# Routing attention and a snake MLP on one core: the first head's one-hot rows made by TensorE, and the preparation of the first pairs dealt out anew

## The chip, the core and the metric

The kernel runs on one core of one Trainium2 chip. The metric is the time of one execution on the device in microseconds (us).

The engines have short names in the profile. PE is TensorE's matmuls, PEld its weight loads, DVE is VectorE, ACT is ScalarE, POOL is GpSimd, and SP is the queue that issues DMAs. "PE S L358" is line 358 of a kernel writing a tile S. The change adds lines near the top of the file, so the same statement has another line number before and after:

| statement | before | after |
|---|---|---|
| scores, two matmuls | L326, L327 | L358, L359 |
| exp | L332 | L364 |
| probabilities times v | L341 | L373 |
| scaling of the attention output to `xs` | L353 | L385 |
| hidden layer | L425 | L457 |
| output layer | L394 | L426 |
| transposes of q and k; their copies by DVE and by ACT | L144; L150, L154 | L144; L150, L154 |
| copies of one-hot rows, by ACT and by DVE | none | L337, L339 |

## The reference, cut to what matters

```python
batch, n_heads, seq, head_dim = (4, 8, 768, 64); n_clusters = 16
q_assign = argmax(einsum('bhsd,hcd->bhsc', q_n, c_n)); k_assign = argmax(...)   # normalised
mask   = q_assign[:, :, :, None] == k_assign[:, :, None, :]
scores = where(mask, scale * q @ k.T, -1e9)
attn   = softmax(scores) @ v                  # x: (3072, 512)
h = x @ w_in                                  # 512 -> 2048
s = sin(alpha * h); g = h + s * s / (alpha + 1e-9)
out = g @ w_out                               # 2048 -> 512
```

Every query and key is assigned to the nearest of 16 centroids. A query sees only the keys of its own cluster.

## The kernel before

The kernel works on 16 pairs of heads, four per batch. A pair takes 12 steps: one block of 128 keys of one head each. A step is a scores product on PE, an exp on ACT, and the product with v on PE. After 48 steps the batch changes to its second part, the MLP, with Sin instead of exp. The next batch's attention follows.

The mask costs no instruction in the loop. Below the 64 rows of q and k in the tile `QK`, 16 rows hold the one-hot assignment, and the scores product adds them. Making these rows is the preparation of a pair. It consists of four PE transposes of q and k, four copies to `T32`, an assignment product, a transpose on DVE, a maximum, a comparison that gives `oh`, a transpose back and DMA moves into `QK`.

```python
def prep_T(m, g, bk=None, eng="dve"):        # one of four: head g//2, q or k
    for jj in range(NJ2):
        nc.tensor.transpose(out=bk[:, P * jj : P * jj + P], ...)          # L144
    if eng == "dve":
        nc.vector.tensor_scalar_mul(out=s["T32"][:, g, :], ...)           # L150
    else:
        nc.scalar.activation(out=s["T32"][:, g, :], ..., func=Copy)       # L154

def head_move(m, h, engs):                   # one-hot rows of one head into QK by DMA
    for g in range(4):
        engs[t].dma_start(out=QK[D : D + NHC, ...], in_=s["ohT"][...])
```

The entry handles pair 0 head by head, so that the first scores start early. Pair 1's transposes follow in the time in which the first head's moves are on the way:

```python
    head_asn(0, 0, M0)
    prep_cast(0, 0)
    for i in range(4):
        prep_hot(0, i, QS)
    prep_T(0, 2, SA[0][:, 0:512], "act")
    prep_T(0, 3, M1, "act")
    head_move(0, 0, [nc.sync, nc.scalar])
    ...
    head_move(0, 1, [nc.sync, nc.sync])
    prep_T(1, 0, M2, "act")
    prep_T(1, 2, M1)
    prep_T(1, 1, M0, "act")
    prep_T(1, 3, OB)
```

Everything else of batch 0 is placed at a step by a table. A row holds the pair, its four transposes with their steps, the step of its assignment, and the steps of its two casts:

```python
    for m, make, asn, cast in (
        (1, (), 1, (0, 0)),
        (2, ((0, 4), (2, 5), (1, 6), (3, 7)), 8, (7, 8)),
        (3, ((0, 12), (1, 14), (2, 16), (3, 17)), 20, (14, 18)),
        ...
```

The change of part, with the transpose `x_T` of the last pair's output, is the same in all four batches:

```python
        hidden_mm(0, A[0], KX - 2, KX - 1)
        hidden_mm(1, A[1], 0, KX - 1)
        x_T(last, OB)
        hidden_mm(2, A[2], 0, KX - 1)
        own = [(1, OB, 3), (0, M0, 5)]       # output products: tile, bank, lag in steps
        for f in range(NF):
            ...
```

The softmax here doesn't subtract the row's maximum and nothing guards it: scores larger than these inputs give would overflow.

## Time and profile before

The median is 312.23 us in the three runs given with the kernel (311.94 to 313.45). The profiled execution spans 310.5 us.

The page's table of engines: busy time, share of the span, and instructions.

```profile
PE 302.7 (97%) x2750; PEld 180.0 (58%) x2750; DVE 208.6 (67%) x367; ACT 239.7 (77%) x324; POOL 139.3 (45%) x222
```

The list of PE's waits, cut to two: engine, tile and line, what was waited for, us in total, times, longest.

```profile
PE S L326 <- DMA QK<-ohT: 1.2, 2, 0.9
PE S L425 <- DVE gT L450: 0.6, 1, 0.6
```

PE is the engine with no room. Its two visible waits that a schedule could remove are the DMA that brings the first one-hot rows (0.9 us, and 0.35 us for pair 1's) and one at the change of part.

The entry in PE's timeline of the kernel before (start us, us busy, what, count, and in brackets the idle time before it with what ended it):

```profile
9.99 0.49 PE L144 MATMUL OB<-ident_f,k 128*128 128x128 f32 x3
10.32 0.38 PE L501 MATMUL S<-gT 128*128 128x512 bf16 x1
11.57 0.38 PE L326 MATMUL S<-QK 80*128 80x512 bf16 x1 [0.86 <-DMA QK<-ohT]
```

The first scores start at 11.57 us, when the DMA has landed.

### The profile page before, as it was taken

The numbers are of one execution on the slowest core, as the hardware profiler recorded it, in microseconds if no ns is written. First come the engines' busy times: TensorE is split into PE (matmuls) and PEld (weight loads), VectorE is DVE, ScalarE is ACT, GpSimd is POOL, SyncE is SP. The second block draws the span as 40 slices with busy tenths as digits, with TensorE's granted clock in tenths as the row PEclk, the third lists the DMA queues.
The fourth block names the chain that finished last, engine by engine and source line by source line (L and its number), as shares of the span: only waits on it lengthen the run. The fifth ranks groups of instructions, "written<-read, shape, count | busy, mean of one in ns | idle before, by whom it ended". The sixth has DMA issues, their size and how long they took to land.

```text
span 310.5 us, 7224 instructions
## 1 busy us (share of the span) xinstructions
PE 302.7 (97%) x2750; PEld 180.0 (58%) x2750; DVE 208.6 (67%) x367; ACT 239.7 (77%) x324; POOL 139.3 (45%) x222
## 2 busy tenths in 40 slices
PE   8899999999999999999999999999999999999995
PEld 4467766455456656555556556555556666555544
DVE  3787796698866876687967877687836312677821
ACT  5689989787689998688679998687679999687300
POOL 5879999019405099985006079990001090000000
PEclk9999999999999999999999999999999999999999
DMA  7459999949653578881044576520011111000031
GB/s 234 142 164 288 310 205 183 200 76 304 219 142 78 116 183 187 256 317 53 0 119 113 104 171 140 143 84 2 0 68 50 37 43 45 6 28 2 0 135 68
DMA packets 28673, 38.91 MB, mean 125 GB/s; under 512 B 5072, under 2 KB 22496, under 8 KB 28640
## 3 DMA queue, kind: packets, MB, share of 16 engines
q0 software_dynamic: 10240, 21.11, 25.9%
q1 hardware_dynamic: 18160, 17.30, 20.6%
q8 instruction: 21, 0.34, 0.4%
q10 hardware_dynamic: 240, 0.06, 0.1%
q14 instruction: 12, 0.10, 0.1%
HBM read 27.30 MB, written 6.29 MB: 108 GB/s over the span
## 4 chain that ended last, share of the span: by engine, by line
PE 87%; ACT 5%; DVE 4%; DMA 2%; issue 1%; SPq 0%; ACTq 0%; DVEq 0%
PE M L394 19%; PE S L425 17%; PE S L326 13%; PE OB L341 10%; PE M L425 8%; PE S L327 6%; PE OB L394 5%; PE M L214 3%; ACT pT L332 3%; PE S L394 2%; DMA QK<-ohT 2%; PE M L144 2%; DVE gT L450 2%; ACT s_sb L438 1%; DVE u_sb L446 1%; PE S L501 1%
## 5 line engine op out<-in xcount | busy, mean ns | idle before, releaser
L332 ACT ACTIVATE pT<-S 128x768 bf16<-128x768 f32 x192 | 143.7, 810 | 15.9 <-PE S L327 14.7
L394 PE MATMUL M<-w_out_bf,gT 128*128 128x512 bf16 (+1 forms) x288 | 90.7, 373 | 0.2
L326 PE MATMUL S<-QK 80*128 80x512 bf16 x192 | 72.9, 380 | 1.5 <-DMA QK<-ohT 1.2
L425 PEld LDWEIGHTS <-w_in_bf 128*128 128x128 bf16 x512 | 49.3, 98 | 37.9 <-issue 1.8
L341 PEld LDWEIGHTS <-pT 128*128 128x128 bf16 x1152 | 56.1, 97 | 21.2 <-ACT pT L332 0.4
L425 PE MATMUL S<-xT,w_in_bf 128*128 128x512 bf16 x352 | 65.0, 326 | 0.7 <-DVE gT L450 0.6
L341 PE MATMUL OB<-VX,pT 128*128 128x65 bf16 x1152 | 61.3, 193 | 0.4 <-ACT pT L332 0.3
L438 ACT ACTIVATE s_sb<-S,alpha_col 128x768 bf16<-128x768 f32 (+2 forms) x45 | 39.4, 886 | 23.7 <-PE S L425 16.1
L394 PEld LDWEIGHTS <-gT 128*128 128x128 bf16 x400 | 38.9, 97 | 30.7 <-issue 5.4
L191 POOL TENSOR_SCALAR QK<-T 64x384 bf16<-64x384 f32 x64 | 35.3, 552 | 37.4 <-DMA T<-Tq 33.4
L327 PE MATMUL S<-QK 80*128 80x256 bf16 x192 | 51.9, 270 | 0.0
L450 DVE SCALAR_TENSOR_TENSOR gT<-u_sb,ralpha,S 128x768 bf16<-128x768 bf16 (+2 forms) x45 | 44.7, 996 | 10.0 <-ACT u_sb L443 7.1
L387 POOL DMA_DIRECT2D xT<-xq x48 | 25.8, 546 | 29.0 <-DVE xq L379 28.1
L425 PE MATMUL M<-xT,w_in_bf 128*128 128x512 bf16 (+1 forms) x160 | 29.9, 326 | 0.0
L186 POOL CAST QK<-T 64x768 bf16<-64x768 f32 x32 | 26.9, 842 | 6.4 <-ACT T L154 3.8
L352 DVE RECIPROCAL rec<-OB 128x6 f32<-128x6 f32 x32 | 6.2, 193 | 34.7 <-PE OB L341 34.7
L446 DVE TENSOR_TENSOR u_sb<-s_sb 128x768 bf16<-128x768 bf16 (+2 forms) x41 | 23.7, 579 | 7.0 <-ACT s_sb L438 7.0
L327 PEld LDWEIGHTS <-QK 80*128 80x128 bf16 x192 | 18.8, 98 | 16.0 <-issue 1.8
L203 POOL CAST VX<-v 128x768 bf16<-128x768 f32 x16 | 13.8, 862 | 28.6 <-issue 27.7
L438 ACT ACTIVATE s_sb<-M,alpha_col 128x512 bf16<-128x512 f32 (+1 forms) x40 | 20.9, 574 | 7.2 <-PE M L425 7.2
L450 DVE SCALAR_TENSOR_TENSOR gT<-u_sb,ralpha,M 128x512 bf16<-128x512 bf16 (+1 forms) x40 | 22.8, 611 | 5.2 <-ACT u_sb L443 4.8
L394 PE MATMUL OB<-w_out_bf,gT 128*128 128x512 bf16 (+1 forms) x80 | 26.2, 358 | 0.1
(83 smaller groups left out, 283.0 us busy)
## 6 DMA issues: line engine op xcount, KB each, us to landing
T<-Tq SPq DMA_DIRECT2D x64, 96.0 KB, 2.5
out_dram<-o_sb SPq DMA_DIRECT2D x23, 256.0 KB, 2.1
v<-in_v_dram POOLq DMA_DIRECT2D x14, 384.0 KB, 4.3
q<-in_q_dram POOLq DMA_DIRECT2D x13, 384.0 KB, 5.5
k<-in_k_dram POOLq DMA_DIRECT2D x13, 384.0 KB, 6.3
w_in_bf<-in_moe_w_in_dram POOLq DMA_DIRECT2D x4, 512.0 KB, 7.2
w_out_bf<-in_moe_w_out_dram POOLq DMA_DIRECT2D x4, 512.0 KB, 9.3
xT<-xq POOLq DMA_DIRECT2D x48, 24.0 KB, 2.3
```

The source lines that it names most:

```text
L186: nc.gpsimd.tensor_copy(out=QK[0:D, m % NQK, h, :, HS * par : HS * par + HS], in_=src)
L191: nc.gpsimd.tensor_scalar(out=QK[0:D, m % NQK, h, t].rearrange("c (n i a) -> c i n a", i=4, a=32)[:, 2 * par : 2 * par + 2], in0=src[:, t] ...
L326: nc.tensor.matmul(out=dst[:, 0:512], lhsT=lhsT, rhs=T[:, 0, 0:512], start=True, stop=True)
L327: nc.tensor.matmul(out=dst[:, 512:S], lhsT=lhsT, rhs=T[:, 0, 512:S], start=True, stop=True)
L332: nc.scalar.activation(out=pT, in_=area(i)[:, 0:S], func=ACTF.Exp, scale=escale)
L341: nc.tensor.matmul(out=o3[:, j, :], lhsT=pT[:, P * j : P * j + P], rhs=VX[m % NVX][:, h, jof(m // NHP, kt), :], start=(kt == 0 and j == 0) ...
L387: nc.gpsimd.dma_start(out=xT[32 * g : 32 * g + 32, 0:2, QS * i : QS * i + QS], in_=xq[0].rearrange("p (h g n) -> p h g n", h=2, g=4)[32 * ...
L394: nc.tensor.matmul(out=bk[:, lo:hi], lhsT=gT[:, f, P * mt : P * mt + P], rhs=w_out_bf[:, f, lo:hi], start=(f == 0), stop=(f == NF - 1),)
L425: nc.tensor.matmul(out=ar[lo // 512][:, 0 : hi - lo] if isinstance(ar, tuple) else ar[:, lo:hi], lhsT=lhsT, rhs=xT[:, kk, :].rearrange("c ...
L438: nc.scalar.activation(out=s_sb[:, lo:hi], in_=src, func=ACTF.Sin, scale=alpha_col[:, f : f + 1])
L446: nc.vector.tensor_tensor(out=u_sb[:, lo:hi], in0=s_sb[:, lo:hi], in1=s_sb[:, lo:hi], op=ALU.mult)
L450: nc.vector.scalar_tensor_tensor(out=gT[:, f, lo:hi], in0=u_sb[:, lo:hi], scalar=ralpha[:, f : f + 1], in1=src, op0=ALU.mult, op1=ALU.add,)
```

## The change

The intent is to start the first scores earlier. PE turns pair 0's first one-hot rows itself, and ACT and DVE copy them into `QK`. The two DVE transposes and the DMA with its wait are gone. The warm-up product that filled this wait goes too. Pair 1 is now handled head by head over steps 0 to 8 and no longer in the entry, so the rest of the table moves back. At the change of part the last pair's `x_T` goes forward, and bank OB's lag in batch 0 becomes 4. The diff, cut to its core:

```diff
-        dense = m < NPE and W == HS
+        dense = m < NPE and W == HS and m != 2        # pair 2: the other layout, four moves
+    def head_rows(m, h, bks):          # 12 PE transposes of oh, then six copies
+        for par in range(2):
+            ... nc.tensor.transpose(out=bk[...], in_=oh[:, par, i, 0:NHC], identity=ident_b)
+        put(0, 0, both, 0, n, "act")
+        put(1, 0, 0, 0, 4, "dve")
+        put(0, 1, both, 0, n, "dve")
+        put(1, 0, 0, 4, n, "act")
+        put(1, 0, 1, 0, n, "act")
+        rows_late[0] = lambda: put(1, 1, both, 0, n, "dve")
...
-    warmup(2)
+    warmup(1)
-    for i in range(4):                 # the two DVE transposes were the fourth
+    for i in range(3):
         prep_hot(0, i, QS)
-    head_move(0, 0, [nc.sync, nc.scalar])
-    load_qk(2)
+    load_qk(2, eng=nc.gpsimd)
+    head_rows(0, 0, (M2, M0))
...
-    head_move(0, 1, [nc.sync, nc.sync])
-    prep_T(1, 0, M2, "act")
-    prep_T(1, 2, M1)
-    prep_T(1, 1, M0, "act")
-    prep_T(1, 3, OB)
+    head_move(0, 1, [nc.sync, nc.gpsimd])
+    rows_late[0]()
+    prep_T(1, 0, M1)
-    warmup(1)                          # the product that filled the wait
...
+    for h, a, bk in ((0, 4, M1), (1, 8, M0)):      # pair 1 head by head
+        at(a, ...head_asn(1, h, bk), prep_hot 0, 1); at(a + 1, ...prep_hot 2, 3, head_move(1, h, ...))
+        at(1 + 6 * h, lambda h=h: prep_cast(1, h))
+    for g, bk, i in ((1, M2, 0), (2, M0, 5), (3, M2, 6)):
+        at(i, lambda g=g, bk=bk: prep_T(1, g, bk))
-        (1, (), 1, (0, 0)),
-        (2, ((0, 4), (2, 5), (1, 6), (3, 7)), 8, (7, 8)),
-        (3, ((0, 12), (1, 14), (2, 16), (3, 17)), 20, (14, 18)),
+        (2, ((0, 7), (2, 10), (1, 11), (3, 12)), 14, (11, 13)),
+        (3, ((0, 16), (2, 17), (1, 18), (3, 19)), 20, (18, 20)),
   ... pairs 4 to 6 one to three steps later; x_T of pair 0 from step 18 to 24, of pair 2 from 43 to 46;
      loads of pair 3 from step 5 to 7 and of pair 4 from 10 to 9
-        hidden_mm(1, A[1], 0, KX - 1)
+        hidden_mm(1, A[1], 0, KX - 2)
         x_T(last, OB)
-        hidden_mm(2, A[2], 0, KX - 1)
-        own = [(1, OB, 3), (0, M0, 5)]
+        hidden_mm(1, A[1], KX - 2, KX - 1)
+        hidden_mm(2, A[2], 0, 1)
+        own = [(1, OB, 3 if b else 4), (0, M0, 5)]
...
+            if f == 0:
+                hidden_mm(2, A[2], 1, KX - 1)
```

## The prediction

> **What bounds it now.** The table of engines has TensorE (PE) busy for 302.7 of 310.5 us; the list of PE's waits holds under 4 us, nearly all in the entry. Three places can give time.
>
> 1. *Entry.* In the timeline the one-hot rows of pair 0's first head are ready on VectorE (DVE) at 8.17 us. Two 32x32 transposes (0.64 us) and a DMA follow; the chain of waits shows PE's first scores at 11.57 us, held by "DMA QK<-ohT", 2.1 us (ScalarE queue) and a median of 3.2 us (SyncE queue) from issue to landing. [...] First exp: 12.09 us.
> 2. *Step 12*, pair 1's first: PE waits 0.35 us at 21.84 us for "DMA QK<-ohT", issued from 16.0 us on.
> 3. *Batch 0's change to the second part.* The last pair's transpose starts at 54.45 us, its input ready at 54.14; the first Sin starts 2.2 us late, at 56.28; PE waits 0.61 us for gT and shortly for ScalarE's copy out of bank OB (60.37).
>
> Between 12 and 52.8 us PE is busy 39.7 of 40.8 us; ScalarE (ACT) needs 38.7 for 48 exps (0.81 each): nearly level, little room.
>
> **What the change does, costed.**
> - Away: two DVE transposes (0.64), the first DMA (about 2.6 us of waiting), one warm-up matmul (about 0.2).
> - New: 12 small PE transposes, about 0.66 us (the six of the x transpose took 0.33). Then copies out of PSUM: ACT 16x384 (about 0.45; 384 columns took 0.49), then DVE copies of 128 and 384 columns, which the built program makes wait for ACT's[...]. Rows ready 7.95, first bank 8.5, ACT 8.95, DVE 9.6; PE also has head 1's assignment and one q transpose in front (until 9.8). First scores at about **9.8** instead of 11.57.
> - Moved: three of pair 1's transposes (0.36 us each, 1.1 us), hidden in the DMA wait before, now lie in steps 0 to 6. Pair 1's first head needs four moves, not eight: landed near 19.7 us, about when step 12 is reached. DVE gets crowded at steps 8 to 10: PE may wait 0.5 us for T32 copies and xs. Steps 13 to 47 carry about 0.9 us more PE work.
> - Batch 0's change of part: x transpose about 0.35 us earlier, OB wait gone (0.1 to 0.2). Batches 1 to 3 show no PE wait there: nothing gained.
>
> **Sum.** Entry -1.7, step 12 -0.35, change of part -0.45, more work in PE-bound steps +0.6: about -1.9 us. Predicted **310.4 us**, 8 in 10 between **309.3** and **311.6**. Faster by over 2% (6.2 us): 0.01; within 2%: 0.98; slower: 0.01. The entry is too short for 2%.
>
> **What would show it right.** First scores at 9.5 to 10.2 us, released by DVE's copy or PE's own queue, not a DMA; first exp near 10.3; step 12's scores at 19.7 to 20.5; last exp of batch 0 ends 51.0 to 51.6 (before 52.76); first Sin 1.5 to 2.2 us earlier than 56.28; then the same pace, shifted.
>
> **What would make it wrong.** Strided 16-partition copies from PSUM slower than estimated; head 1's moves on the GpSimd queue landing after 14.4 us, so that step 6 waits; DVE crowding costing over 1 us; the later pairs' transposes making steps 14 to 47 PE-bound, giving back the gain.

The sum: -1.7 - 0.35 - 0.45 + 0.6 = -1.9 us. The times "first bank 8.5, ACT 8.95, DVE 9.6" are my estimates. In the changed kernel's trace ACT's copy took 0.47 us, and DVE's two took 0.49 us together where the estimate gives them 0.65.

## More of the kernel before

The next view is the table of stretches of the kernel before. Each line holds the stretch, its length, the busy us of the five engines with their instruction counts, the clock, and the DMA. I cut at the starts of the scores of steps 0, 4, 12, 18, 24 and 30.

```profile
11.56:14.49 2.93, 2.86 (x29) 1.26 (x29) 1.60 (x4) 2.37 (x4) 2.77 (x4) 1.00 0.83 279
14.49:21.84 7.35, 7.00 (x86) 4.86 (x85) 6.52 (x12) 6.51 (x9) 5.76 (x8) 1.00 0.57 176
21.84:26.59 4.75, 4.69 (x60) 3.71 (x61) 3.18 (x9) 4.41 (x7) 4.70 (x7) 1.00 0.62 183
26.59:31.92 5.33, 5.33 (x73) 3.70 (x71) 4.53 (x10) 4.75 (x7) 5.15 (x8) 1.00 1.04 293
31.92:36.66 4.74, 4.68 (x65) 3.69 (x63) 3.36 (x8) 4.56 (x7) 4.65 (x7) 1.00 1.06 331
```

DVE, the third number after the length, is busy 3.18 of 4.75 us in steps 12 to 18 and 4.53 of 5.33 us in steps 18 to 24. That second figure is 85%.

## The result, and the profile after

The changed kernel takes 312.69 us (median of six runs, 312.66 to 313.09). The kernel before takes 312.40 us beside it (311.94 to 313.61, six runs). The ratio is 1.0005, with a 95% interval from 0.9983 to 1.0027. Ratios here are the mean time of one kernel's runs over the mean of the kernel before's runs in the same rounds, so they are not quite the ratios of the medians. The change gives nothing: it is 2.3 us from the predicted 310.4 and outside the range.

The profiled span is 310.8 us (310.5 before). The table of engines of the changed kernel:

```profile
PE 303.6 (98%) x2768; PEld 179.3 (58%) x2768; DVE 209.7 (67%) x377; ACT 240.6 (77%) x325; POOL 140.9 (45%) x227
```

The list of PE's waits, cut to two lines that are new:

```profile
PE S L358 <- DVE QK L339: 0.7, 1, 0.7
PE M L326 <- DVE oh L263: 0.5, 1, 0.5
```

The waits for the DMA and for `gT` are gone, as intended. PE's entry now:

```profile
8.87 0.55 PE L144 MATMUL M<-ident_f,q 128*128 128x128 f32 x3
9.41 0.38 PE L358 MATMUL S<-QK 80*128 80x512 bf16 x1
```

and further down:

```profile
11.98 0.39 PE L358 MATMUL S<-QK 80*128 80x512 bf16 x1 [0.70 <-DVE QK L339]
```

The first scores start at 9.41 us, 2.16 us earlier than before. At 11.98 us PE waits 0.70 us for DVE's last copy of one-hot rows.

To see where the lead goes, I follow the start of the exp of a step on ACT, and the first Sin, in both traces (us; the difference is after minus before):

| | before | after | difference |
|---|---|---|---|
| exp of step 0 | 12.09 | 9.93 | -2.16 |
| step 12 | 22.42 | 20.53 | -1.89 |
| step 18 | 27.18 | 25.82 | -1.35 |
| step 24 | 32.51 | 32.01 | -0.51 |
| step 28 | 35.54 | 35.40 | -0.14 |
| step 47, the last of batch 0 | 51.96 | 51.81 | -0.15 |
| first Sin | 56.28 | 55.59 | -0.69 |
| second exp of batch 1 | 85.98 | 85.66 | -0.32 |
| first exp of batch 2 | 154.42 | 154.12 | -0.30 |
| third exp of batch 3 | 228.33 | 228.22 | -0.11 |
| end of the span | 310.46 | 310.84 | +0.38 |

The lead is real and is gone by step 28. A second gain of 0.54 us at the change of part is given back in pieces by the end. The table of stretches of the changed kernel, cut at the same steps:

```profile
9.41:12.68 3.27, 2.51 (x24) 1.34 (x24) 3.03 (x8) 2.56 (x5) 2.88 (x5) 1.00 0.56 219
12.68:19.94 7.26, 7.15 (x101) 5.04 (x98) 6.11 (x17) 6.49 (x9) 4.96 (x8) 1.00 0.29 70
19.94:25.24 5.30, 5.30 (x68) 3.45 (x66) 4.46 (x12) 4.72 (x7) 5.24 (x8) 1.00 0.97 307
25.24:31.42 6.18, 6.13 (x70) 3.76 (x68) 5.81 (x13) 4.92 (x7) 6.00 (x9) 1.00 0.93 252
31.42:36.53 5.11, 4.92 (x70) 3.87 (x70) 3.58 (x8) 4.56 (x7) 4.95 (x8) 1.00 0.99 269
```

Subtracting the lengths gives the loss by stage:

| steps | loss, us |
|---|---|
| 0 to 4 | 0.34 |
| 4 to 12 | -0.09 |
| 12 to 18 | 0.55 |
| 18 to 24 | 0.85 |
| 24 to 30 | 0.37 |
| sum | 2.02 |

In steps 18 to 24 DVE is busy 5.81 of 6.18 us (94%, before 85%), PE 6.13 and GpSimd 6.00. All three look full, so the table alone cannot say which one binds. DVE's timeline in this stage:

```profile
22.96 0.58 DVE L243 STREAM_TRANSPOSE asT<-M 128x384 f32<-128x384 f32 x1
23.58 0.55 DVE L246 TENSOR_REDUCE amax<-asT 128x24 f32<-128x384 f32 x1
24.17 0.91 DVE L263 TENSOR_TENSOR oh<-asT,amax 128x384 bf16<-128x384 f32 x1
25.11 1.04 DVE L283 STREAM_TRANSPOSE ohT<-oh 128x384 bf16<-128x384 bf16 x2
26.07 1.91 DVE L150 TENSOR_SCALAR T<-M 128x384 f32<-128x384 f32 x4
```

ACT's timeline, the line at which ACT has to wait longest:

```profile
29.40 2.37 ACT L364 ACTIVATE pT<-S 128x768 bf16<-128x768 f32 x3 [0.79 <-PE S L359]
```

DVE goes from pair 2's one-hot rows to four `T32` copies without a gap, and these four copies feed pair 3's assignment on PE. That assignment shows 1.24 us of busy time on PE, where those of pairs 2, 4 and 5 show 0.85. It consists of eight small products: normally one gap of 0.33 us lies between their starts, here there are two, of 0.33 and 0.35. So a group that is held half way counts as busy. (The expectations of e7 and e11 below speak of 0.66 us more; these busy times give 0.39.) ACT then idles 0.79 us, since the scores behind the assignment are late.

### The profile page after: what moved, and what is told of

It reads as the page before. It is cut to its first block, busy times and chain, and to the rows that moved or that the text cites. A ratio compares the mean times of both kernels' runs of the same rounds, so it can differ in the third digit from the quotient of the medians.

```text
span 310.8 us, 7261 instructions
## 1 busy us (share of the span) xinstructions
PE 303.6 (98%) x2768; PEld 179.3 (58%) x2768; DVE 209.7 (67%) x377; ACT 240.6 (77%) x325; POOL 140.9 (45%) x227
## 4 chain that ended last, share of the span: by engine, by line
PE 85%; DVE 6%; ACT 5%; SPq 1%; issue 1%; DMA 1%; DVEq 0%; ACTq 0%
PE M L426 19%; PE S L457 17%; PE S L358 12%; PE OB L373 10%; PE M L457 8%; PE S L359 6%; PE OB L426 5%; PE M L214 3%; ACT pT L364 3%; PE S L426 2%; PE M L144 2%; DVE gT L482 2%; SPq L295 1%; DMA QK<-ohT 1%; ACT s_sb L470 1%
## 5 line engine op out<-in xcount | busy, mean ns | idle before, releaser
L457 PE MATMUL S<-xT,w_in_bf 128*128 128x512 bf16 x352 | 66.2, 326 | 0.0
L457 PE MATMUL M<-xT,w_in_bf 128*128 128x512 bf16 (+1 forms) x160 | 30.6, 326 | 0.0
L203 POOL CAST VX<-v 128x768 bf16<-128x768 f32 x16 | 13.5, 844 | 28.6 <-issue 27.7
```

The source lines that it names most:

```text
L457: nc.tensor.matmul(out=ar[lo // 512][:, 0 : hi - lo] if isinstance(ar, tuple) else ar[:, lo:hi], lhsT=lhsT, rhs=xT[:, kk, :].rearrange("c ...
```

## The experiments

Fifteen kernels ran. Each was compared with the kernel before on the same chip.

| run | what it is | median us | before | ratio, 95% interval |
|---|---|---|---|---|
| e1_part_change_only | before, new change of part | 312.63 | 312.35 | 1.0019 (0.9997 to 1.0040) |
| e2_entry_only | after, old change of part | 313.05 | 312.35 | 1.0025 (1.0010 to 1.0040) |
| e3_order_b0 | after, new order in batch 0 only | 312.91 | 312.35 | 1.0013 (0.9999 to 1.0028) |
| e4_skip_after | after, three transposes of pair 1 left out | 312.80 | 312.35 | 1.0009 (0.9994 to 1.0024) |
| e5_loads_later | after, later loads | 312.64 | 312.27 | 1.0012 (0.9998 to 1.0026) |
| e6_loads_later_skip | e4 and e5 together | 313.91 | 312.27 | 1.0053 (1.0021 to 1.0085) |
| e7_asn3_later | after, pair 3's assignment a step later | 313.08 | 312.27 | 1.0028 (1.0015 to 1.0042) |
| e8_three | e3, e5 and e7 together | 313.20 | 312.27 | 1.0030 (1.0017 to 1.0042) |
| e9_skip_pair3 | e5, pair 3's transposes left out | 312.75 | 312.36 | 1.0009 (0.9992 to 1.0026) |
| e10_skip_before | before, e4's transposes left out | 313.95 | 312.36 | 1.0059 (1.0033 to 1.0085) |
| e11_copies_on_act | e5, four copies from DVE to ACT | 311.47 | 312.36 | 0.9969 (0.9952 to 0.9986) |
| e12_before_order_b0 | before, new order in batch 0 only | 311.70 | 312.36 | 0.9978 (0.9963 to 0.9992) |
| e13_copies_only | after, four copies from DVE to ACT | 312.02 | 312.32 | 0.9989 (0.9971 to 1.0008) |
| e14_copies_order_b0 | e11 with e12's order | 311.53 | 312.32 | 0.9978 (0.9959 to 0.9997) |
| e15_milder_loads | e14, loads less late | 311.58 | 312.32 | 0.9990 (0.9966 to 1.0014) |

The expectations below were written before each run. They name theories by letters, as the texts spell them out. The two that matter most are D and F. D says that the one-hot rows' moves land late because of loads in flight. F says that DVE takes the lead back. The plain rival is that PE's own moved work does it. None of the runs differs from the kernel before by as much as 2%; what is compared is fractions of a us. A profile is one execution: those of e3, e10, e11, e13 and e15 were the fastest of their runs, those of e6 and e14 the slowest.

Up to the last exp of batch 0, e2 and e3 have the same code as the changed kernel. Their profiles so show what chance does there: that exp starts at 51.81 us in the changed kernel, 52.48 in e2 and 51.57 in e3. Nearly all of it arises in steps 18 to 24, which take 6.18, 6.87 and 6.02 us. A difference of that size between two profiles needs a second witness.

### The two halves of the change apart: e1, e2, e3

The edit of e1 is the last part of the diff above (change of part and lag) put alone into the kernel before. e2 is the rest alone.

> The kernel before with nothing but the new order at the change to the second part (x transpose earlier, bank OB one step later), in all four batches. Theory A (from the two traces): in batch 0 the first Sin comes 0.4 to 0.6 us earlier after the last exp, because PE, ScalarE and VectorE wait for each other there; in batches 1 to 3 PE has filler work, so the earlier x transpose only makes PE wait about 0.2 us for the copy of x each time, and batch 1's second exp comes about 0.35 us later after its first. Sum within 0.3 us of the kernel before. Rival B (my prediction): 0.45 us faster, batches 1 to 3 untouched.

> The changed kernel with the old order at the change to the second part: entry and plan of batch 0 alone. Theory A: the first scores start near 9.4 us (2.2 us earlier than before), but the last exp of batch 0 ends within 0.3 us of the kernel before, and the whole within 0.4 us of it. Rival B (my prediction's entry term): batch 0's last exp at least 1 us earlier, the whole 1 to 2 us faster than before.

e1's profile has the first Sin 0.54 us earlier, the second exp of batch 1 only 0.17 us earlier, and the end 0.17 us later. ACT's idle time at the start of batch 1 explains the first return. Batches are numbered from 0. These lines of ACT's timeline are the second and third exp of batch 1, of the kernel before and then of e1:

```profile
85.98 1.51 ACT L332 ACTIVATE pT<-S 128x768 bf16<-128x768 f32 x2 [1.98 <-PE S L327]
```

```profile
85.81 1.51 ACT L332 ACTIVATE pT<-S 128x768 bf16<-128x768 f32 x2 [2.36 <-PE S L327]
```

With a lag of 4, one more output product into OB, and one more of the products that fill up behind it, are left for the start of batch 1, so PE reaches the scores 0.38 us later. In batches 1 to 3 the first Sin comes 0.41 us earlier against the last exp, and nine Sins later this is given back: the sums are -0.03, +0.18 and -0.03 us. The new order is worth nothing there.

e2 starts its exps 1.85 us earlier than the kernel before. It is 0.28 us later than the kernel before at step 24, where PE's list of waits shows 0.7 us for "DMA QK<-ohT", and its last exp is 0.52 us later. The line of that list:

```profile
PE S L358 <- DMA QK<-ohT: 0.7, 1, 0.7
```

So even the entry alone, with its lead of 1.85 us, loses it before step 24.

```diff
-        hidden_mm(1, A[1], 0, KX - 2)
+        hidden_mm(1, A[1], 0, KX - (1 if b else 2))
         x_T(last, OB)
-        hidden_mm(1, A[1], KX - 2, KX - 1)
-        hidden_mm(2, A[2], 0, 1)
+        if b == 0:
+            hidden_mm(1, A[1], KX - 2, KX - 1)
+        hidden_mm(2, A[2], 0, KX - 1 if b else 1)
```

> The changed kernel with the new order at the change to the second part in batch 0 alone, the old order in batches 1 to 3. Theory A: each of batches 1 to 3 no longer loses its 0.2 us there; the whole is 0.4 to 0.7 us faster than the changed kernel, about 312.1 us. Rival B (the drift of 0.7 us after batch 1 is chance, such as stalls and store landing): the whole equals the changed kernel within 0.15 us.

e3 keeps the new order only where PE waited, in batch 0 (with the lag of 4). The profiled span falls to 310.5 us (it was the fastest of its five runs), but the five timed runs show no gain over the changed kernel (312.91 against 312.69, from different rounds). Batch 1's start still costs 0.37 us, because of the lag.

### PE's moved work, the rival: e4, e6, e9, e10

Three of pair 1's transposes were hidden in the DMA wait before, and now lie in steps 0 to 6. e4 leaves them out on PE. Its results are wrong; two banks are cleared first so that nothing is read uninitialised.

```diff
-        for jj in range(NJ2):
+        for jj in range(0 if m == 1 and g > 0 else NJ2):
```

> The changed kernel without the matrix-engine half of three of pair 1's four transposes (those that moved into steps 0 to 6); the copies stay and read stale banks, so the result is wrong on purpose. Theory A (batch 0's steps are bound by PE's work, so every moved transpose costs its full 0.36 us): batch 0's last exp ends 0.8 to 1.2 us earlier than in the changed kernel (52.6 us), the whole 0.8 to 1.2 us faster. Rival C (the lead is lost in waits for VectorE at steps 3, 9 and 20 and the transposes fit in PE's gaps): last exp earlier by less than 0.3 us.

e4 is 0.32 us further ahead than the changed kernel at step 12. Step 13 then waited 0.8 us for one of pair 1's moves, whose issue alone took 1.56 us where most take 0.59 (the longest in the changed kernel took 2.19). The last exp is at -0.06 us against the kernel before, later than the changed kernel's -0.15. Nothing is gained by step 47 without these transposes. Because of the stall at step 13 this alone is a weak proof against the rival; e9 is the stronger one.

> The same later loads, and in addition three of pair 1's transposes left out on PE (wrong result on purpose). In the run without them alone, batch 0's last exp stood 0.1 us later than in the changed kernel, not 1 us earlier. Theory D: it was held at step 13 and step 24 by landings; with step 24's gone, the last exp ends 0.5 to 1 us earlier than with the later loads alone, unless pair 1's moves hold step 13 again. Theory A: 0.9 to 1.1 us earlier. If it is again within 0.2 us, the transposes are not the cost.

e6 (also wrong) says nothing on this question, but shows something else. In this line of its table of stretches the clock is the third number from the end:

```profile
11.68:18.50 6.82, 6.60 (x55) 4.24 (x56) 3.82 (x10) 4.11 (x6) 3.15 (x5) 0.50 0.25 70
```

For 6.82 us TensorE ran at half its clock. By the same table PE had been busy only 3.07 us of the 4.68 before that; its longest idle time up to then, once its work had begun, was 0.78 us, around the fall of the clock. What set the clock back is not shown. Two of e6's four runs took 314.98 us and two 312.7 to 312.8. The run is inconclusive.

> The kernel before, with the same three transposes of pair 1 left out on PE that were left out in the changed kernel (wrong result on purpose). In the kernel before they stand in the wait for the first DMA of one-hot rows. Theory A: they cost nothing there; first scores (11.56 us) and last exp of batch 0 (51.96 us) within 0.15 us of the kernel before, apart from the start of the full clock.

e10 leaves the same three transposes out of the kernel before. They only filled a wait there. The first scores start at 11.59 us (11.56 before), and the last exp is 0.34 us later: at step 12 PE waited 0.7 us for pair 1's moves, where it had waited 0.35. Its spread up to 315.02 us makes the times unusable.

e9 takes the rival directly: it leaves out all four transposes of pair 3 on PE, in e5's form of the kernel (next section), while the DVE copies stay.

```diff
-        for jj in range(NJ2):
+        for jj in range(0 if m == 3 else NJ2):
```

> The changed kernel with the later loads, and pair 3's four transposes left out on PE (wrong result on purpose; the copies stay). They stand at steps 16 to 19, where PE is busy 99 to 100% of the time. Compare with the later loads alone, where step 24's scores start at 31.34 us and the last exp of batch 0 at 51.90 us. Theory A (PE's work binds here): 1.0 to 1.44 us earlier (4 x 0.36 us) at step 24 and at the last exp. Theory F (VectorE, 94% busy over steps 18 to 24, binds): less than 0.4 us.

The stretches of steps 12 to 18 and 18 to 24 of e5, which has the transposes, and then of e9:

```profile
20.03:25.32 5.29, 5.29 (x68) 3.45 (x66) 4.45 (x12) 4.71 (x7) 5.17 (x8) 1.00 0.94 296
25.32:31.34 6.02, 5.97 (x70) 3.76 (x68) 5.65 (x13) 4.76 (x7) 4.93 (x7) 1.00 0.40 110
```

```profile
20.00:25.02 5.02, 4.90 (x63) 2.94 (x60) 4.22 (x11) 4.49 (x7) 4.90 (x8) 1.00 0.99 314
25.02:31.34 6.32, 5.96 (x62) 3.43 (x62) 5.92 (x14) 4.63 (x7) 5.23 (x7) 1.00 0.36 98
```

With 1.44 us of PE work gone, step 18 comes 0.30 us earlier, and step 24 comes at 31.34 us in both. The 0.30 us are lost again behind DVE, which is busy 5.92 of 6.32 us: its four copies end at 28.1 us as in the changed kernel (28.0), and pair 3's assignment now waits openly for one of them and shows 1.76 us of busy time. The line of PE's waits in e9:

```profile
PE M L214 <- DVE T L150: 0.3, 1, 0.3
```

The rival falls for steps 12 to 24 taken together, as long as DVE has these copies. The rival holds only in part for steps 12 to 18 alone, where e9's stage is 0.27 us shorter than e5's. No run took PE's work away with the copies on ACT.

### The loads and the moves: e5

In the changed kernel pair 2's moves were issued at 26.18 to 28.04 us and landed 4.0 to 5.0 us later, at 31.16 to 32.06; step 24's scores, which need them, start at 31.42. Loads (pair 5's q and k, a v, and from 27.7 us the first piece of w_in) were in flight. e5 delays loads that have time:

```diff
-    for m, i in {4: 9, 5: 12, 6: 18, 7: 22}.items():
+    for m, i in {4: 9, 5: 18, 6: 20, 7: 24}.items():
-        (15, load_w_in, 0),
+        (22, load_w_in, 0),
```

> The changed kernel; only the loads of pairs 5 to 7 and the first piece of w_in are issued later, so that none is in flight with the moves of pair 2's one-hot rows. Theory D (seen in the first runs: step 24's scores start 0.1 to 0.4 us after pair 2's first two moves land, at 31.2 to 32.3 us, whatever happened before): the moves, issued from 26.2 us on, land within 2 to 3 us instead of 4 to 5, step 24's scores start near 30.8 us instead of 31.42, and batch 0's last exp ends 0.2 to 0.6 us earlier than in the changed kernel. Theory A (PE's work alone binds steps 13 to 28): moves land earlier, steps unchanged within 0.15 us.

The moves now took 1.9 to 3.2 us and landed at 29.48 to 30.67 us, 1.4 to 1.7 us earlier. Step 24 started at 31.34 us, 0.08 us earlier. Theory D by itself falls: with the moves there in time, something else held step 24. As a second limit the landing is real, though. In the changed kernel, e2 and e13, step 24's first scores start 0.09 to 0.10 us after the second move has landed (31.33, 32.12 and 30.89 us), and 0.54, 1.22 and 0.54 us after the transpose in front of them has started. In the other fourteen profiles that last distance is 0.36 us. So the landing cost 0.18, 0.86 and 0.18 us there, and nothing in e3, which has the early loads too. In the kernel before, pair 0's first moves (12 KB each) landed 1.8 to 2.2 us after issue, pair 2's eight of the same size 1.7 to 6.0 us. Why moves take longer beside loads is not shown: no run here separates the causes.

### DVE: e7, e8, e11, e13

e7 puts pair 3's assignment one step later, so that it need not wait for the copies.

```diff
-        (3, ((0, 16), (2, 17), (1, 18), (3, 19)), 20, (18, 20)),
+        (3, ((0, 16), (2, 17), (1, 18), (3, 19)), 21, (18, 20)),
```

> The changed kernel with pair 3's assignment one step later (21 instead of 20), two steps after its last transpose. In the trace of the changed kernel PE stood in that assignment 0.66 us longer than elsewhere, waiting for VectorE's copy of the last transpose, and ScalarE was idle 0.79 us at step 21. Theory E (that wait is part of what gave the lead back): step 22's exp starts 0.3 to 0.6 us earlier than in the changed kernel; if theory D holds too, the landing of pair 2's moves at step 24 takes it back, and the last exp ends within 0.2 us of the changed kernel.

The exp of step 21 comes 0.94 us earlier than in the changed kernel. Then PE's list of waits, from 9 to 53 us, has a new first line:

```profile
PE OB L373 <- DVE xs L385: 1.1, 2, 0.7
```

PE waits for DVE's `xs`, and the exp of step 24 is 0.26 us and that of step 28 0.46 us later than in the changed kernel. DVE's work is in a row; where PE meets it is a matter of order.

> A mended version: later loads, pair 3's assignment at step 21, the new order at the change to the second part in batch 0 alone. Theories D and E with the loss of batches 1 to 3: batch 0's last exp ends 0.6 to 1.2 us earlier than in the changed kernel, the whole 1 to 1.7 us faster than the changed kernel and about 1 us faster than the kernel before. If PE's work alone binds (theory A), only the 0.6 us of batches 1 to 3: equal to the kernel before.

e8 joins e3, e5 and e7, and shows the same new wait (1.2 us). It is no better than e7.

e11 takes work off DVE: in e5's kernel, four of DVE's `T32` copies go to ACT, two of pair 1 (where ACT had two before the change) and two of pair 3.

```diff
-        at(i, lambda g=g, bk=bk: prep_T(1, g, bk))
+        at(i, lambda g=g, bk=bk: prep_T(1, g, bk, "dve" if g == 1 else "act"))
...
-            at(i, lambda g=g: prep_T(m, g))
+            at(i, lambda g=g: prep_T(m, g, None, "act" if m == 3 and g in (0, 2) else "dve"))
```

> The changed kernel with the later loads, and four of VectorE's copies of transposes (two of pair 1, two of pair 3; 0.52 us each) moved to ScalarE, which has 10 to 20% idle time in these steps. Theory F: steps 4 to 24 together take 0.5 to 1.5 us less than with the later loads alone (7.26 + 5.30 + 6.02 us); pair 3's assignment no longer waits for a copy. Theory A: PE's work is unchanged, so at most the 0.66 us wait in that assignment goes, and steps 4 to 18 stay within 0.1 us.

The result is correct, and 311.47 us (four runs, 311.40 to 311.62): the ratio to the kernel before is 0.9969, the best of all, and its interval ends below 1. The last exp of batch 0 is 0.86 us ahead of the kernel before. The stretches of steps 12 to 18 and 18 to 24 of e11:

```profile
19.50:24.80 5.30, 5.30 (x69) 3.45 (x67) 4.47 (x10) 4.77 (x8) 5.18 (x8) 1.00 0.92 299
24.80:30.42 5.62, 5.60 (x71) 3.87 (x68) 5.05 (x11) 5.08 (x9) 5.04 (x7) 1.00 0.41 118
```

Steps 18 to 24 fall from 6.02 us in e5 to 5.62, with the same transposes on PE. Pair 3's assignment takes 0.94 us instead of 1.24. Steps 4 to 12 gain a little too (7.14 against 7.26). Steps 12 to 18 do not change: there PE is busy 5.30 of 5.30 us, as in the changed kernel, with pair 2's assignment and more moved into them.

Not all of e11's lead is the copies' doing. Its last exp is 0.80 us ahead of e5's, but 0.41 of that is there at step 4, before the first moved copy; 0.12 come in steps 4 to 12 and 0.40 in steps 18 to 24, and 0.12 are lost after step 36. And of the 1.17 us between the two medians, 0.5 us may belong to two stalls in batches 1 and 3 that are absent with the copies on ACT (point 6 below).

The next two views are e11's groups for the two forms of the same copy, first by ACT and then by DVE, with count, and shortest, median and longest ns:

```profile
L154 ACT ACTIVATE T<-M x7: 485/491/525, 4.4 to 25.4; 128x384 f32<-128x384 f32 x7
```

```profile
L150 DVE TENSOR_SCALAR T<-M x23: 518/557/558, 11.6 to 48.9; 128x384 f32<-128x384 f32 x23
```

So four copies are about 2.2 us of DVE's time, about 1.1 of it before step 12. ACT makes the same copy in a median of 491 ns (485 to 525) where DVE takes 557 (518 to 558).

e13 leaves the loads as they were and moves only the copies.

> The changed kernel with only the four T copies moved from VectorE to ScalarE (pair 1 g 2 and 3, pair 3 g 0 and 2), loads as in the changed kernel. F (VectorE alone took the entry's lead back): step 18 to 24 in about 5.6 us as in e11, last exp of batch 0 about 0.8 us earlier than the changed kernel's, total about 311.5. F with D as a second limit (pair 2's moves, which land late while loads are in flight, bind as soon as VectorE does not): the moves are issued earlier but land at 31.2 to 32 us, step 24's scores stay at 31.0 to 31.4, the last exp is at most 0.3 us earlier than the changed kernel's, total about 312.3.

e13 ends at 312.02 us, and its interval includes 1; the profile, the fastest of its five runs, has the last exp 0.65 us ahead of the kernel before (after: 0.15, e11: 0.86). Steps 18 to 24:

```profile
25.18:30.98 5.80, 5.77 (x70) 3.83 (x68) 5.23 (x11) 5.27 (x9) 5.62 (x8) 1.00 0.93 259
```

This stage can be laid out as a two by two table, in us. Before the change it took 5.33.

| | loads as in the change | loads later |
|---|---|---|
| copies on DVE | 6.18 (e2: 6.87, e3: 6.02) | 6.02 (e5) |
| four copies on ACT | 5.80 (e13) | 5.62 (e11, e14, e15) |

Where the landing does not hold step 24 (see e5), the stage takes 6.02 us with the copies on DVE (e3, e5) and 5.62 with them on ACT (e11, e14, e15): the copies are worth 0.40 us. The landing adds 0.18 us in the changed kernel and in e13, 0.86 in e2 and nothing in e3. So what the early loads cost varies from run to run, and the table's 0.16 to 0.18 is not their fixed price. What keeps e11's 5.62 us above the 5.33 of the kernel before is not known: PE is busy 5.60 of them. GpSimd, as full as PE in the changed kernel (6.00 us), is not the limit: in e5 it is busy 4.93 us, and the stage takes the 6.02 us of e3. The expectation of e13 gave DVE alone 5.6 us, and DVE with the moves as a hard second limit at most 0.3 us by the last exp. It came in between (0.50), so the sharp form of both is wrong. In e13 the first head's moves of pair 2 landed at 30.70 and 30.89 us and the scores started at 30.98, which is the 0.09 us after a landing that the changed kernel and e2 show too. PE's list of waits names no DMA there, but the start came 0.18 us later than the transpose in front allows. So F with D as a second limit was right in kind and too strong in size.

### What beats both: e12, e14, e15

e12 is the kernel before with e3's order in batch 0, and the lag of 3 kept.

> The kernel before with only the new order of x transpose and hidden blocks, in batch 0 alone, and the old lag of bank OB. A candidate to beat both. In the run of the new order in all batches the first Sin of batch 0 came 0.54 us earlier, and batches 1 to 3 lost about 0.2 us each. Expected: 0.3 to 0.5 us faster than the kernel before, about 311.9 us. If the gain is lost again at batch 1's start (a wait of ScalarE), 0 to 0.2 us.

It takes 311.70 us (six runs, 311.50 to 312.18), ratio 0.9978. The first Sin is 0.58 us earlier, and all of it is still there at the second exp of batch 1 (-0.57) and at the end (-0.55). This is the one gain of the change that holds by itself to the end.

> e11 with the new order of the change of part in batch 0 alone and bank OB's lag of 3 kept (as e12). If the pieces add: batch 0 of e11 (last exp 51.1, about 0.85 before the kernel before), first Sin as before or 0.1 better, no extra out matmul at batch 1's start (exp 49 0.3 earlier than e11's), batches 1 to 3 not slowed by 0.2 each (0.6 in all): 310.6 us, range 310.2 to 311.1, ratio to before about 0.9945.

> e14 with pairs 6 and 7 and the first piece of w_in loaded one, two and two steps earlier. If e11's stall of 0.40 us at step 39 comes from GpSimd, whose loads of late steps pushed pair 3's cast of v: about 0.2 us faster than e14; if pair 2's moves are hit by these loads again, step 24 is later than 30.5 and the time is that of e14 or worse. Range 310.2 to 311.2.

e14 is e11 with e12's order and lag. e15 is e14 with pairs 6 and 7 loaded at steps 19 and 22 and the first piece of w_in at 20. The expected 310.6 us did not come: the medians are 311.53 and 311.58 us, no better than e11. In e14's profile, the slowest of its five runs (312.21 us), PE waited 1.1 us at 9.83 us for the load of pair 1's q, so its lead was only 1.35 us at the first exp, and its last exp is level with the kernel before's. e15's profile has no such wait. At the second exp of batch 1 it is 1.22 us ahead of the kernel before, where e11 is 1.03 us ahead; at the end the two are 0.89 and 0.83 us ahead. The lag of 3 pays at batch 1's start, and two stalls that the kernel before does not have eat it: 0.32 us between the third and the tenth Sin of batch 2, and 0.24 us after the last store (point 6 below). The expectation of e14 also counted on 0.6 us from batches 1 to 3. That was a misreading of single stalls: from the second exp of batch 1 to a late Sin of batch 3, e11 takes 0.05 us less than the kernel before with the new order in these batches, and e15 takes 0.10 us more with the old one. That the pieces do not add up in the timed runs is measured; the cause of the first stall stays open.

## Why the prediction was wrong

In the two profiles the sum is -2.16 us (entry), +2.02 (steps 0 to 30), -0.54 (change of part), +0.37 (start of batch 1) and +0.70 (from there to the end), about +0.4 us. The prediction had -1.7 for the first, +0.25 for the second (+0.6 of work, -0.35 at step 12), -0.45 for the third, and nothing for the last two. Point by point:

1. **The entry, -1.7 us: right, and even more.** The first scores start at 9.41 us instead of the predicted 9.8, and the exp is 2.16 us earlier. About 0.3 us of that may be the clock: full clock began at 5.74 us in this profile and at 7.24 in that of the kernel before. In e2, which has the same entry and where it began at 7.19, the lead is 1.85. The order of the copies held as well. Here are the first copies of one-hot rows in the changed kernel, from ACT's timeline and then from DVE's:

```profile
8.31 0.47 ACT L337 COPY QK<-M 16x384 bf16<-16x384 bf16 x1 [0.43 <-PE M L326]
```

```profile
8.81 0.49 DVE L339 COPY QK<-M 16x128 bf16<-16x128 bf16 x2 [1.10 <-ACT QK L337]
```

   DVE starts at 8.81 us, when ACT is done (8.31 + 0.47 = 8.78), and the trace puts its 1.10 us of idle time down to ACT's copy. Why the built program has this wait is not shown.

2. **"More work in PE-bound steps +0.6": this is the step that failed, by size and by engine.** It should have been about 2.0 us (the table of losses). I had counted PE's extra work, and had noted that DVE might be crowded at steps 8 to 10, by 0.5 us, without adding this to the sum. The crowding came later and was larger. With e11 and e13 it is shown that moving 2.2 us of copies from DVE shortens steps 18 to 24 by 0.4 us and steps 4 to 12 by 0.1. With e9 it is shown that removing 1.44 us of PE work (four transposes of 0.36) gains nothing by step 24. So about 0.5 of the 2.0 us is shown to be DVE's, and 0.18 was the late landing. The rest is argued or open.
   DVE had got more to do in the first 28 steps, about 3.3 us by my count of its instructions in the two traces: pair 1 head by head (0.8), pair 2 in the longer layout (0.5), three copies of one-hot rows (0.9), and two copies of pair 1 that had been ACT's (1.1). It had also lost some (the two transposes of the entry, and a copy of pair 5 that now comes later), so that its busy time up to step 28's exp is 26.41 us against 25.00.
   The 0.34 us of steps 0 to 4 also stand behind DVE: PE's 0.70 us wait for its late copy of rows. No run was made to take that wait away, so what it is worth by the end is not known. The 0.55 us of steps 12 to 18 look like PE's (busy throughout, work moved in), about the size that I had given; e9, which leaves out two transposes of that stage, shortened it by 0.27 us only, so this is argued. Of the 0.85 us of steps 18 to 24, 0.27 remain with copies and landing out of the way, cause open. The 0.37 us of steps 24 to 30 appear in all the changed forms, e9 and e11 too. Pair 0's `x_T` was moved into them; that this is the cause was only argued.

3. **"Step 12 -0.35".** The wait at step 12 is gone, as said. It made no separate gain. Steps 4 to 12 are only 0.09 us shorter, and the sum counted the wait as if PE had nothing else to do by then.

4. **"Last exp of batch 0 ends 51.0 to 51.6".** It ends at about 52.6 (starts at 51.81, takes 0.81), against 52.76 before. This is where the trace first contradicts the prediction.

5. **Change of part, -0.45: right in batch 0** (-0.54 at the first Sin; e12: -0.58), but the same edit's lag of 4 costs 0.37 us at batch 1's start. "Batches 1 to 3 show no PE wait there: nothing gained" holds: the sums are -0.03, +0.18 and -0.03 us in e1.

6. **What is left.** Some single stalls of 0.2 to 0.3 us come and go between kernels with the same code at that place. All nine traces with the new entry and the copies on DVE (the changed kernel, e2 to e9) lose 0.26 to 0.29 us between the eleventh and the twenty-seventh step of batch 1, and about the same again in batch 3. The four with copies on ACT (e11, e13 to e15) lose nothing there. From one late Sin of batch 3 to the end, the thirteen kernels with the new entry take 19.44 to 19.46 us, and the four with the old entry 19.20 to 19.21; in all seventeen the 0.24 us lie after the last store has landed (1.34 against 1.09 us). The packed traces show what is there: at the end SyncE waits on semaphores in a row, two per instruction and 0.06 us apart, with eight such instructions in the thirteen and four in the four. So this loss belongs to the end of the program and not to its schedule. For the other stalls PE's list of waits names nothing, and their cause stays open. They are of the size of the effects sought, so a profile difference below 0.3 us should not be explained from one pair of traces; in steps 18 to 24 even one of 0.85 us came with a late landing alone (e2 against e3).

## What to carry to other kernels

Here a lead of 2.16 us at the start was down to 0.14 us by step 28, and about 0.5 us of the loss is shown to lie on DVE, where displaced work went: list the added work per engine and per stage before summing. The busy shares did not name the limit: in the stage where the work landed DVE showed 85% before and 94% after, less than PE (100 and 99%) and GpSimd (97 and 97%). An engine that shows full may only be held half way (in the changed kernel pair 3's assignment counts 1.24 us busy on PE, those of pairs 2, 4 and 5 count 0.85), so test by taking work away from one engine at a time, which here named DVE in four traces. Run the same code more than once before explaining a profile. And when a change is applied in a loop over batches, apply it only where the wait was seen; in batches 1 to 3 of e1 it gained 0.41 us at the first Sin and gave it back within nine Sins.
